# Group 0's keys as two transfers by slot, its first slot prepared and scored by itself, and keys ahead of queries in groups 1 and 2

## The chip, the cores and the metric

The kernel runs on one core of one Trainium2 chip. The metric is the device time of one execution in microseconds (us), the median of several runs. A time in the text without another name is a point on the clock of the profiled execution, counted from the start of its span.

## The reference, cut to what matters

Eight batches of twelve heads with 448 positions of 64 numbers go through a sigmoid attention. The result, seen as 3584 rows of 768, goes through two dense layers with a gated sigmoid between them. Inputs and output are fp32 in HBM.

```python
# q, k, v: (8, 12, 448, 64); w_in: (768, 2048); w_out: (2048, 768); beta: (2048,)
scores = q @ k.transpose(0, 1, 3, 2) / sqrt(64) - log(448)
attn   = sigmoid(scores) @ v                         # (8, 12, 448, 64)
x      = attn.transpose(0, 2, 1, 3).reshape(3584, 768)
h      = x @ w_in
g      = h * sigmoid(beta * h)
out    = g @ w_out                                   # (3584, 768)
```

## The kernel before, in words

**Groups, slots and tiles.** The twelve heads of a batch are worked in three groups of four heads (a "quad" in the code; groups 0, 1 and 2 are batch 0). The 128 partitions of a group's tile hold its four heads, 32 partitions each. A slot is a pair of heads, 64 partitions, so slot 0 of group 0 is the upper half of the tile and slot 1 the lower half. The 448 keys of a head are three key tiles of 128 (`jt` 0 to 2) and a last one of 64 (`jt` = `JF` = 3). In code, `NB` = 14 is the number of 32-position columns, `NH` = 7 is half of them, and `NF` = 12 is the columns of the three full tiles.

**Way of the data.** `load_one` (L106, its DMA at L110) brings a group's queries (`r` = 0) or keys (`r` = 1) by a DMA that GpSimd (POOL) issues and that casts to fp16 on the way. `transpose` (L186) has VectorE (DVE) transpose them in 32x32 blocks: queries at L191, the three full key tiles at L199, the last key tile at L203. `score` (L210, L213) multiplies them on TensorE (PE), `weigh` (L222, L224) applies the sigmoid on ScalarE (ACT), and `attend` (L270) multiplies with the values, which DVE casts out of PSUM at L290. `dense1` (L295) is the first dense layer: matmuls at L166 (the line of a helper for all dense matmuls), sigmoid at L307, product at L310. `dense2` (L321) is the second. The values come by `load_v` (L131 and L138), w_in in eight chunks by `load_w_in` (L148), w_out in four by `load_w_out` (L156). Chunk c of w_in holds what `dense1` needs for `dc` = 2c and 2c + 1. The first transfer of w_out serves parts 0 to 3 of the first `dense2`, that is its first eight matmuls, and the second transfer the next eight.

**The start, which the change touches.** Everything up to the first dense layer is in an order written out by hand (L509 on); each engine runs its instructions in that order. Group 0 is not cast by a DMA. SyncE (SP) issues two plain fp32 transfers at L519, the first half of the queries and then all keys, into a piece of the tile `gt` that is not yet in use. DVE casts the queries (L539) and transposes them; ACT casts the second half of the keys (L541) and DVE the first half (L542); DVE transposes all keys (L199, L203). Meanwhile PE multiplies zeros: `idle_units` (L533) issues matmuls of 512 columns whose result nobody reads, nine of them ahead of the first scores (L537), and four (two in the last group) between one half visit and the next (L563). A half visit (L252) is the scores of half of the queries of a group, for two slots: the first one of a group does key tiles 0 and 1 (16 matmuls, two sigmoids), the second one tile 2 and the last tile (16 matmuls, two sigmoids). Within a half visit the matmuls of the two slots alternate. There are three PSUM tiles for scores.

**POOL's order of transfers.** After a memset of `dummy` (L525): group 1's first query half, group 1's keys, the same two of group 2, four transfers of values (L131), two of values (L138), the second query half of group 0, that of group 1, chunks 0 to 3 of w_in, the second query half of group 2, chunks 4 to 7 of w_in. Later come group 3's queries and keys, two transfers of w_out and the values of batch 1. From the ninth transfer on, each one is issued only when the eighth one before it has landed, because eight semaphores take turns.

**After the start.** `attend`, `half_visit` and `fill_units` alternate (L564 on); `fill_units` takes the next units of the dense layers from a list. The transpose of group 2's second query half stands ahead of `attend(0, QH, QH)` in the code (L592), and the half visit that needs it, `half_visit(2, QH, 0)`, stands behind one dense unit (L594, L595).

Of the kernel before, what the change touches and what calls it, by code (L numbers as in the profile page):

```python
# [8 lines left out]
FP32 = mybir.dt.float32  # L9
FP16 = mybir.dt.float16  # L10
# [3 lines left out]
def kernel(  # L14
# [10 lines left out]
    nc = tc.nc  # L25
# [3 lines left out]
    B, H, S, D = q.shape  # L29
    NTOK, DM = out.shape  # L30
    DFF = moe_w_in.shape[1]
    P = 128
    BLK = 32
    HQ = P // BLK
    NB = S // BLK
    PAIR = D // BLK
    JF = S // P
    KL = S - JF * P
    NF = JF * P // BLK
    NPAIR = H // 2  # L40
    QPB = H // HQ
# [15 lines left out]
    kTp = ctx.enter_context(tc.tile_pool(name="kTp", bufs=4))  # L57
# [34 lines left out]
    dummy = const.tile([P, 1], FP32, name="dummy")  # L92
# [10 lines left out]
    raws = {}  # L103
    vs = {}

    def load_one(g: int, r: int, c0: int = 0, c1: int = NB):  # L106
        b, t = divmod(g, QPB)
        if g not in raws:
            raws[g] = rawp.tile([P, 2, NB, D], FP16, tag="raw", name="raw")
        nc.gpsimd.dma_start(  # L110
            out=raws[g][:, r, c0:c1].rearrange("p c d -> p (c d)"),
            in_=(q, k)[r][b, HQ * t : HQ * (t + 1)].rearrange("h (p c) d -> (h p) (c d)", c=NB)[
                :, c0 * D : c1 * D
            ],
        )
# [11 lines left out]
    def load_v(b: int):  # L127
        vs[b] = vp.tile([P, H, JF + 1, D], FP16, tag="v16", name="v16")
        rows = v[b].rearrange("h (p c) d -> p h (c d)", c=NB)
        for i in range(HQ):  # L130
            nc.gpsimd.dma_start(  # L131
                out=vs[b][i * BLK : (i + 1) * BLK, :, 0:JF].rearrange("p h j d -> p h (j d)"),
                in_=rows[:, :, JF * i * D : JF * (i + 1) * D],
            )
        rows = v[b].rearrange("h (p c) d -> p h c d", c=NB)
        for c in range(NF, NB):
            lo = (c - NF) * BLK
            nc.gpsimd.dma_start(out=vs[b][lo : lo + BLK, :, JF], in_=rows[:, :, c])  # L138

    def double_v_last(b: int):  # L140
        nc.vector.tensor_copy(out=vs[b][KL:P, :, JF], in_=vs[b][0:KL, :, JF])

    WCH = 8
    WOUT = 2

    def load_w_in(c: int):
        n = DFF // WCH
        nc.gpsimd.dma_start(  # L148
            out=w_in16[:, :, c * n : (c + 1) * n],
            in_=moe_w_in[:, c * n : (c + 1) * n].rearrange("(c p) f -> p c f", p=P),  # L150
        )
# [23 lines left out]
    kT = {}  # L175
# [6 lines left out]
    def in_order(b: int, t):  # L182
        t = t.rearrange("p c e -> p (c e)").bitcast(FP32)
        return t.rearrange("p (q c) -> p c q", c=NB) if b == B - 1 else t

    def transpose(g: int, r: int, c0: int = 0, c1: int = NB):  # L186
        raw = raws[g][:, r]
        if r == 0:
            if g not in qT:
                qT[g] = qTp.tile([P, NB * BLK, PAIR], FP16, tag="qT", name="qT")  # L190
            nc.vector.transpose(  # L191
                out=in_order(g // QPB, qT[g][:, c0 * BLK : c1 * BLK]),
                in_=raw[:, c0:c1].rearrange("p c d -> p (c d)").bitcast(FP32),
            )
            return
        kT[g] = kTp.tile([P, S, PAIR], FP16, tag="kT", name="kT")
        to = kT[g].rearrange("p k e -> p (k e)").bitcast(FP32)
        frm = raw.rearrange("p c d -> p (c d)").bitcast(FP32).rearrange("p (c f) -> p c f", c=NB)
        nc.vector.transpose(  # L199
            out=to[:, 0 : JF * P].rearrange("p (j i q) -> p i j q", j=JF, i=HQ),  # L200
            in_=frm[:, 0:NF].rearrange("p (i j) f -> p i j f", j=JF),
        )
        nc.vector.transpose(  # L203
            out=to[:, JF * P :], in_=frm[:, NF:].rearrange("p c f -> p (c f)")
        )

    def score_tile():
        return psum["sc"].tile([P, 2, 512], FP32, tag="sco", name="sco")

    def score(sco, u0: int, s: int, jt: int, hh: int, e: int, c0: int, n: int):  # L210
        g, lo = s // 2, (s % 2 * 2 + hh) * BLK
        base, nk = (last_base(s), KL) if jt == JF else (0, P)
        nc.tensor.matmul(  # L213
            sco[base : base + nk, hh, u0 : u0 + n],
            kT[g][lo : lo + BLK, jt * P : jt * P + nk, e],
            qT[g][lo : lo + BLK, c0 : c0 + n, e],
            start=(e == 0),
            stop=(e == PAIR - 1),
            tile_position=(lo, base),
        )  # L220

    def weigh(sco, n: int):  # L222
        at = attnp.tile([P, 2, S], FP16, tag="attnT", name="attnT")
        nc.scalar.activation(  # L224
            out=at[:, :, 0:n],
            in_=sco[:, :, 0:n],
            func=AF.Sigmoid,
            bias=NEG_LOG_S,
            scale=MSCALE,
        )  # L230
        return at
# [17 lines left out]
                at_tiles[s, jt, 0] = at  # L249


    def half_visit(g: int, c0: int, second: int):  # L252
        slots = (2 * g, 2 * g + 1)
        scos = [score_tile() for _ in slots]
        plan = [(s, jt, sco, jt * QH) for jt in (0, 1) for s, sco in zip(slots, scos)]
        widths = [S, S]
        if second:
            plan = [(s, 2, sco, 0) for s, sco in zip(slots, scos)]
            plan += [(s, JF, scos[0], QH) for s in slots]
            widths = [S, QH]  # L260
        for i in range(0, len(plan), 2):
            for e in range(PAIR):
                for s, jt, sco, u0 in plan[i : i + 2]:
                    for hh in range(2):
                        score(sco, u0, s, jt, hh, e, c0, QH)
        ats = {id(sco): weigh(sco, n) for sco, n in zip(scos, widths)}
        for s, jt, sco, u0 in plan:
            at_tiles[s, jt, c0] = ats[id(sco)][:, :, u0 : u0 + QH]
# [237 lines left out]
    NH = NB // 2  # L506
    firsts = ctx.enter_context(ExitStack())
    share_psum(firsts, 3, 2)
    with tc.manual_schedule():  # L509
        raws[0] = rawp.tile([P, 2, NB, D], FP16, tag="raw", name="raw")  # L510
        wide = gt.rearrange("p a b -> p (a b)").bitcast(FP32)
        cut = NH * D
        early = [(0, 0, NH), (1, 0, NB)]
        staged = {}
        at = 0
        for r, c0, c1 in early:
            staged[r] = wide[:, at : at + (c1 - c0) * D]
            at += (c1 - c0) * D
            nc.sync.dma_start(  # L519
                out=staged[r],  # L520
                in_=(q, k)[r][0, 0:HQ].rearrange("h (p c) d -> (h p) (c d)", c=NB)[
                    :, c0 * D : c1 * D
                ],
            )
        nc.gpsimd.memset(dummy, 0.0)  # L525
        nc.scalar.activation(out=dummy, in_=dummy, func=AF.Sigmoid, bias=0.0, scale=1.0)

        still = const.tile([P, 512], FP16, name="still")
# [4 lines left out]
        def idle_units(n: int):  # L533
            for _ in range(n):
                nc.tensor.matmul(idle, still[:, 0:P], still, start=True, stop=True)

        idle_units(9)  # L537
        raw = raws[0].rearrange("p r c d -> p r (c d)")
        nc.vector.tensor_copy(out=raw[:, 0, 0:cut], in_=staged[0])  # L539
        transpose(0, 0, 0, NH)  # L540
        nc.scalar.copy(out=raw[:, 1, cut:], in_=staged[1][:, cut:])  # L541
        nc.vector.tensor_copy(out=raw[:, 1, 0:cut], in_=staged[1][:, 0:cut])  # L542
        transpose(0, 1)
        for g in range(1, QPB):
            load_one(g, 0, 0, NH)
            load_one(g, 1)
        load_v(0)
        nc.sync.dma_start(out=beta_in[0:NDC], in_=moe_beta.rearrange("(c p) -> c p", p=P))
        for g in range(QPB - 1):
            load_one(g, 0, NH, NB)  # L550
        for c in range(WCH):
            if c == WCH // 2:
                load_one(QPB - 1, 0, NH, NB)
            load_w_in(c)
        for g in range(1, QPB):
            transpose(g, 0, 0, NH)
            transpose(g, 1)

        for g in range(QPB):
            for second in range(2):  # L560
                half_visit(g, 0, second)
                if 2 * g + second < 2 * QPB - 1:
                    idle_units(4 if g < QPB - 1 else 2)  # L563
        double_v_last(0)  # L564
        transpose(0, 0, NH, NB)
        attend(0, 0, QH)
        half_visit(0, QH, 0)
        attend(1, 0, QH)
        half_visit(0, QH, 1)
        for g in range(1, QPB - 1):  # L570
            transpose(g, 0, NH, NB)
# [128 lines left out]
```

## Time and profile before

| what | us |
|---|---|
| median of three runs | 383.44 |
| the three runs | 382.74 to 384.87 |
| the profiled execution | 383.27 |
| its span in the profile | 381.5 |
| PE busy | 375.9 (99% of the span) |
| DVE busy | 231.9 (61%) |
| ACT busy | 229.2 (60%) |
| POOL busy | 66.4 (17%) |

The span runs from the first instruction to the last; 1.77 us of the profiled execution lie around it. PE's busy time counts the matmuls on zeros as well. In a timeline row the first number is the start, the second the length, then engine, source line, operation, output and input tiles, shapes and how often; in brackets stands how long the engine had been idle and what ended that. A row that ends in x8 merges eight instructions of one kind, with the small gaps between them. PEld is TensorE's weight load, which runs beside its matmuls. SPq and POOLq are the queues that issue transfers.

### The profile page before, as it was taken

The page shows a single profiled execution, that of the slowest core. Times are in us where ns is not written, and L with a number is a line of the kernel's source. Part 1 is how long each engine was busy: PE and PEld are TensorE (multiplying, and loading weights), DVE is VectorE, ACT ScalarE, POOL GpSimd, SP SyncE. Part 2 cuts the span into 40 slices and gives each one's busy share as a digit, 9 for nine tenths or more (in the row PEclk, how much of TensorE's full clock was granted, in tenths as well). Part 3 has the DMA queues.
Part 4 walks back from the last instruction along what each step waited for, and adds up shares of the span by engine and source line. Part 5 has one row for each costly group of instructions (what it writes and reads, how often), then busy time and mean ns, then how long its engine had stood idle before and what let it go on. Part 6 is the DMA issues. An engine that isn't in the chain of part 4 may idle for free.

```text
span 381.5 us, 8227 instructions
## 1 busy us (share of the span) xinstructions
PE 375.9 (99%) x3415; PEld 199.0 (52%) x3415; DVE 231.9 (61%) x439; ACT 229.2 (60%) x330; POOL 66.4 (17%) x114
## 2 busy tenths in 40 slices
PE   8999999999999999999999999999999999999996
PEld 3477744444654445444554445544455444555563
DVE  4357366775765557465775657665676665755761
ACT  5987756687356776577355792477752787435100
POOL 7842433140110410040110410112100000000000
PEclk9999999999999999999999999999999999999999
DMA  9999999755363930672363850649203300030033
GB/s 169 187 197 205 192 204 210 164 71 54 50 132 84 121 51 2 131 98 24 50 132 72 115 69 2 133 87 117 50 0 84 85 1 2 2 83 0 2 83 125
DMA packets 42405, 34.71 MB, mean 91 GB/s; under 512 B 21872, under 2 KB 38656, under 8 KB 42368
## 3 DMA queue, kind: packets, MB, share of 16 engines
q0 software_dynamic: 36688, 22.47, 43.5%
q1 hardware_dynamic: 5680, 11.71, 11.6%
q8 instruction: 27, 0.44, 0.5%
q14 instruction: 10, 0.08, 0.1%
HBM read 45.62 MB, written 11.01 MB: 148 GB/s over the span
## 4 chain that ended last, share of the span: by engine, by line
PE 88%; DMA 9%; POOL 1%; issue 0%; DVE 0%; POOLq 0%
PE m_ps L166 70%; PE sco L213 10%; PE av_ps L281 8%; DMA w_out<-in_moe_w_out_dram 5%; DMA w_in<-in_moe_w_in_dram 3%; DMA raw<-in_k_dram 2%; POOL w_in L148 1%; POOL raw L110 1%; POOL w_out L156 0%; DVE osb L342 0%; POOL dummy L525 0%; POOLq L684 0%
## 5 line engine op out<-in xcount | busy, mean ns | idle before, releaser
L224 ACT ACTIVATE attnT<-sco 128x896 f16<-128x896 f32 (+1 forms) x171 | 145.3, 902 | 81.2 <-PE sco L213 80.6
L166 PE MATMUL m_ps<-xT,w_in 128*128 128x448 f16 (+2 forms) x1014 | 154.7, 336 | 0.1
L310 DVE TENSOR_TENSOR gt<-m_ps,sg 128x448 f16<-128x448 f32 (+1 forms) x144 | 81.4, 572 | 81.1 <-ACT sg L307 77.6
L166 PEld LDWEIGHTS <-w_in 128*128 128x128 f16 (+1 forms) x1014 | 82.6, 101 | 68.8 <-issue 15.0
L307 ACT ACTIVATE sg<-m_ps,beta_sb 128x448 f32<-128x448 f32 (+1 forms) x144 | 84.2, 597 | 36.5 <-PE m_ps L166 29.5
L166 PEld LDWEIGHTS <-sum 128*64 128x64 f16 (+1 forms) x664 | 48.0, 104 | 33.6 <-issue 7.9
L213 PE MATMUL sco<-qT,kT 32*128 32x448 f16 (+3 forms) x864 | 51.9, 340 | 0.7 <-DVE kT L199 0.6
L166 PE MATMUL m_ps<-w_T,sum 128*128 128x384 f16 (+1 forms) x360 | 51.6, 327 | 0.0
L110 POOL DMA_DIRECT2D raw<-in_q_dram x26 | 14.3, 552 | 184.1 <-DVE kT L203 176.9
L430 DVE TENSOR_TENSOR osb<-m_ps,osb 128x384 f32<-128x384 f32 x60 | 33.3, 555 | 18.7 <-PE m_ps L166 16.9
L166 PEld LDWEIGHTS <-gt 128*128 128x128 f16 (+1 forms) x414 | 31.4, 103 | 24.0 <-issue 6.5
L281 PE MATMUL av_ps<-attnT,v 128*64 128x448 f16 (+3 forms) x432 | 40.2, 338 | 0.0
L400 DVE TENSOR_TENSOR sum<-gt 128x1024 f16<-128x1024 f16 x60 | 39.2, 678 | 0.1
L290 DVE CAST xT<-av_ps 128x448 f16<-128x448 f32 (+1 forms) x54 | 28.5, 568 | 15.2 <-PE av_ps L281 14.1
L166 PE MATMUL m_ps<-w_T,gt 128*64 128x384 f16 (+1 forms) x268 | 34.3, 327 | 0.0
L166 PE MATMUL m_ps<-w_out,sum 128*64 128x384 f16 (+1 forms) x304 | 33.8, 327 | 0.0
L281 PEld LDWEIGHTS <-v 128*64 128x64 f16 (+1 forms) x432 | 20.6, 108 | 18.8 <-issue 9.4
L213 PEld LDWEIGHTS <-kT 32*128 32x128 f16 (+1 forms) x864 | 13.7, 96 | 28.6 <-issue 26.0
L166 PE MATMUL m_ps<-w_out,gt 128*128 128x384 f16 (+3 forms) x146 | 22.7, 327 | 0.1
L131 POOL DMA_DIRECT2D v<-in_v_dram x32 | 19.8, 631 | 9.6 <-DMA w_in<-in_moe_w_in_dram 5.2
L191 DVE STREAM_TRANSPOSE qT<-raw 128x448 f32<-128x448 f32 (+1 forms) x27 | 16.7, 617 | 0.1
L433 ACT COPY osb<-m_ps 128x384 f32<-128x384 f32 x12 | 5.8, 481 | 16.8 <-DMA out_dram<-osb 8.6
(25 smaller groups left out, 90.0 us busy)
## 6 DMA issues: line engine op xcount, KB each, us to landing
out_dram<-osb SPq DMA_DIRECT2D x98, 96.0 KB, 1.9
raw<-in_k_dram POOLq DMA_DIRECT2D x23, 224.0 KB, 4.9
raw<-in_q_dram POOLq DMA_DIRECT2D x21, 224.0 KB, 3.8
v<-in_v_dram POOLq DMA_DIRECT2D x32, 144.0 KB, 6.7
w_in<-in_moe_w_in_dram POOLq DMA_DIRECT2D x8, 384.0 KB, 11.2
w_out<-in_moe_w_out_dram POOLq DMA_DIRECT2D x4, 768.0 KB, 13.0
v<-in_v_dram POOLq DMA_DIRECT2D x16, 48.0 KB, 6.4
out_dram<-osb SPq DMA_DIRECT2D x2, 384.0 KB, 3.0
```

What stands on the lines that cost most here:

```text
L110: nc.gpsimd.dma_start(out=raws[g][:, r, c0:c1].rearrange("p c d -> p (c d)"), in_=(q, k)[r][b, HQ * t : HQ * (t + 1)].rearrange("h (p c) d ...
L131: nc.gpsimd.dma_start(out=vs[b][i * BLK : (i + 1) * BLK, :, 0:JF].rearrange("p h j d -> p h (j d)"), in_=rows[:, :, JF * i * D : JF * (i + ...
L166: nc.tensor.matmul(to[c : c + step], hidden[:, c : c + step], weights, **({} if step == P else {"tile_position": (0, c)}), **flags,)
L191: nc.vector.transpose(out=in_order(g // QPB, qT[g][:, c0 * BLK : c1 * BLK]), in_=raw[:, c0:c1].rearrange("p c d -> p (c d)").bitcast(FP32),)
L213: nc.tensor.matmul(sco[base : base + nk, hh, u0 : u0 + n], kT[g][lo : lo + BLK, jt * P : jt * P + nk, e], qT[g][lo : lo + BLK, c0 : c0 + n ...
L224: nc.scalar.activation(out=at[:, :, 0:n], in_=sco[:, :, 0:n], func=AF.Sigmoid, bias=NEG_LOG_S, scale=MSCALE,)
L281: nc.tensor.matmul(av[hh * D : (hh + 1) * D, 0:n], vs[b][base : base + nk, 2 * (s % NPAIR) + hh, jt], at[base : base + nk, hh, 0:n], start ...
L290: nc.vector.tensor_copy(out=xTs[b][:, s % NPAIR, c0 : c0 + n], in_=av[:, 0:n])
L307: nc.scalar.activation(out=sg[:, 0:n], in_=m1[:, 0:n], func=AF.Sigmoid, bias=0.0, scale=beta_sb[:, dc : dc + 1])
L310: nc.vector.tensor_tensor(out=gt[:, dc, off : off + n], in0=m1[:, 0:n], in1=sg[:, 0:n], op=ALU.mult)
L400: nc.vector.tensor_tensor(out=sums[t, i], in0=x, in1=y, op=op)
L430: nc.vector.tensor_tensor(out=out, in0=in0, in1=in1, op=op)
```

## The change

The first part concerns group 0. SP now issues three transfers, the queries' first half, the keys of slot 0 (64 partitions) and the keys of slot 1. The casts and transposes of the keys are cut into pieces: ACT casts key tiles 0 and 1 of slot 0 and tile 0 of slot 1, DVE casts tile 1 of slot 1, then tile 2 and the last tile of both slots, with the transposes between. In the first half visit of group 0 all scores of slot 0 come ahead of those of slot 1, and one idle unit stands between them. The idle units at the start become eight, and the four behind the first half visit become two. The memset of `dummy` moves from POOL to DVE.

The second part is the order of POOL's transfers: keys ahead of the queries in groups 1 and 2, and the second query half of group 2 behind chunk 4 of w_in instead of ahead of it. DVE's transposes of groups 1 and 2 follow: full key tiles, queries, last key tile. The instructions behind these places keep their order on every engine.

```diff
+    def transpose_keys(g: int, j0: int, j1: int, rows):
+        if g not in kT:
+            kT[g] = kTp.tile([P, S, PAIR], FP16, tag="kT", name="kT")
+        to = kT[g][rows].rearrange("p k e -> p (k e)").bitcast(FP32)
+        frm = raws[g][rows, 1].rearrange("p c d -> p (c d)").bitcast(FP32)
+        frm = frm.rearrange("p (c f) -> p c f", c=NB)
+        if j0 == JF:
+            nc.vector.transpose(
+                out=to[:, JF * P :], in_=frm[:, NF:].rearrange("p c f -> p (c f)")
+            )
+            return
         nc.vector.transpose(
+            out=to[:, j0 * P : j1 * P].rearrange("p (j i q) -> p i j q", i=HQ, q=BLK),
+            in_=frm[:, 0:NF].rearrange("p (i j) f -> p i j f", j=JF)[:, :, j0:j1],
         )
...
-    def half_visit(g: int, c0: int, second: int):
+    def half_visit(g: int, c0: int, second: int, between=None):
...
-        for i in range(0, len(plan), 2):
+        if between:
+            plan = [x for sco in scos for x in plan if x[2] is sco]
+        step = 1 if between else 2
+        for i in range(0, len(plan), step):
+            if i == 2 and between:
+                between()
             for e in range(PAIR):
-                for s, jt, sco, u0 in plan[i : i + 2]:
+                for s, jt, sco, u0 in plan[i : i + step]:
...
+        by_slot = [slice(x * P // 2, (x + 1) * P // 2) for x in range(2)]
+        nc.sync.dma_start(
+            out=flat(q0),
+            in_=q[0, 0:HQ].rearrange("h (p c) d -> (h p) (c d)", c=NB)[:, 0 : NH * D],
+        )
+        for x, rows in enumerate(by_slot):
             nc.sync.dma_start(
+                out=flat(k0[rows]),
+                in_=k[0, 2 * x : 2 * x + 2].rearrange("h (p c) d -> (h p) (c d)", c=NB),
+            )
-        nc.gpsimd.memset(dummy, 0.0)
+        nc.vector.memset(dummy, 0.0)
...
-        idle_units(9)
+        idle_units(8)
...
-        nc.scalar.copy(out=raw[:, 1, cut:], in_=staged[1][:, cut:])
-        nc.vector.tensor_copy(out=raw[:, 1, 0:cut], in_=staged[1][:, 0:cut])
-        transpose(0, 1)
+        cast_keys(nc.scalar.copy, by_slot[0], 0, 2)
+        transpose_keys(0, 0, 2, by_slot[0])
+        cast_keys(nc.scalar.copy, by_slot[1], 0, 1)
+        cast_keys(nc.vector.tensor_copy, by_slot[1], 1, 2)
+        transpose_keys(0, 0, 2, by_slot[1])
+        every = slice(0, P)
+        cast_keys(nc.vector.tensor_copy, every, 2, JF)
+        nc.vector.tensor_copy(out=raw_k[:, NF:], in_=k0[:, NF:])
+        transpose_keys(0, 2, JF, every)
+        transpose_keys(0, JF, JF + 1, every)
         for g in range(1, QPB):
+            load_one(g, 1)
             load_one(g, 0, 0, NH)
-            load_one(g, 1)
...
         for c in range(WCH):
-            if c == WCH // 2:
+            if c == WCH // 2 + 1:
                 load_one(QPB - 1, 0, NH, NB)
             load_w_in(c)
         for g in range(1, QPB):
+            transpose_keys(g, 0, JF, every)
             transpose(g, 0, 0, NH)
-            transpose(g, 1)
+            transpose_keys(g, JF, JF + 1, every)
...
-                half_visit(g, 0, second)
+                first = 2 * g + second == 0
+                half_visit(g, 0, second, (lambda: idle_units(1)) if first else None)
                 if 2 * g + second < 2 * QPB - 1:
-                    idle_units(4 if g < QPB - 1 else 2)
+                    idle_units(2 if first else 4 if g < QPB - 1 else 2)
```

More of the change, by code (lines that the diff above doesn't have):

```diff
@@ L195, in transpose @@
             return
[L196 to L204, printed above, removed]
+        transpose_keys(g, 0, JF, slice(0, P))
+        transpose_keys(g, JF, JF + 1, slice(0, P))
+    def transpose_keys(g: int, j0: int, j1: int, rows):
[9 more added lines that the diff above has]
+            return
+        nc.vector.transpose(
+            out=to[:, j0 * P : j1 * P].rearrange("p (j i q) -> p i j q", i=HQ, q=BLK),
+            in_=frm[:, 0:NF].rearrange("p (i j) f -> p i j f", j=JF)[:, :, j0:j1],
         )
@@ L511, with flat @@
         wide = gt.rearrange("p a b -> p (a b)").bitcast(FP32)
[L512 to L518, printed above, removed]
+        k0 = wide[:, 0 : NB * D].rearrange("p (c d) -> p c d", c=NB)
+        q0 = wide[:, NB * D : (NB + NH) * D].rearrange("p (c d) -> p c d", c=NH)
+        def flat(t):
+            return t.rearrange("p c d -> p (c d)")
+        by_slot = [slice(x * P // 2, (x + 1) * P // 2) for x in range(2)]
[4 more added lines that the diff above has]
+        for x, rows in enumerate(by_slot):
             nc.sync.dma_start(
[L520 to L523, printed above, removed]
+                out=flat(k0[rows]),
+                in_=k[0, 2 * x : 2 * x + 2].rearrange("h (p c) d -> (h p) (c d)", c=NB),
             )
-        nc.gpsimd.memset(dummy, 0.0)
+        nc.vector.memset(dummy, 0.0)
         nc.scalar.activation(out=dummy, in_=dummy, func=AF.Sigmoid, bias=0.0, scale=1.0)
@@ L535, in idle_units, with by_tile, cast_keys @@
                 nc.tensor.matmul(idle, still[:, 0:P], still, start=True, stop=True)
-        idle_units(9)
-        raw = raws[0].rearrange("p r c d -> p r (c d)")
-        nc.vector.tensor_copy(out=raw[:, 0, 0:cut], in_=staged[0])
-        transpose(0, 0, 0, NH)
-        nc.scalar.copy(out=raw[:, 1, cut:], in_=staged[1][:, cut:])
-        nc.vector.tensor_copy(out=raw[:, 1, 0:cut], in_=staged[1][:, 0:cut])
-        transpose(0, 1)
+        idle_units(8)
+        raw_q, raw_k = raws[0][:, 0], raws[0][:, 1]
+        def by_tile(t, rows, j0: int, j1: int):
+            return t[rows, 0:NF].rearrange("p (i j) d -> p i (j d)", j=JF)[:, :, j0 * D : j1 * D]
+        def cast_keys(copy, rows, j0: int, j1: int):
+            copy(out=by_tile(raw_k, rows, j0, j1), in_=by_tile(k0, rows, j0, j1))
+        nc.vector.tensor_copy(out=raw_q[:, 0:NH], in_=q0)
+        transpose(0, 0, 0, NH)
+        cast_keys(nc.scalar.copy, by_slot[0], 0, 2)
[8 more added lines that the diff above has]
+        transpose_keys(0, JF, JF + 1, every)
         for g in range(1, QPB):
+            load_one(g, 1)
             load_one(g, 0, 0, NH)
-            load_one(g, 1)
         load_v(0)
```

## Prediction

> **What bounds the kernel now.** I read the page's chain of work first. It ends in PE almost everywhere, but a tenth of it is transfers:
>
> ```profile
> PE 88%; DMA 9%; POOL 1%; issue 0%; DVE 0%; POOLq 0%
> ```
>
> The chain cut to the first 60 us tells where these transfers stand (start, length, what):
>
> ```profile
> 2.96 6.43 DMA raw<-in_k_dram
> ...
> 12.70 10.47 DMA w_in<-in_moe_w_in_dram
> 23.18 0.28 issue
> 23.46 0.88 POOL w_out L156
> 24.34 18.36 DMA w_out<-in_moe_w_out_dram
> 42.71 0.04 issue
> 42.75 1.46 PE m_ps L166 x8
> ```
>
> The second transfer of w_out lands at 42.71, and PE goes on at 42.75. From there to the end the chain is PE without a gap, so a shift of the matmuls at 42.75 is the shift of the end. Ahead of 42.7 transfers set the pace. The DMA share by stretches is 0.93 or more in every microsecond from 2 to 5, and at 18.36 us from issue to landing this transfer waited in a long queue. The timelines of POOL, PEld and DVE from 24 to 30 us show a gate on the way:
>
> ```profile
> 25.20 0.40 DVE L191 STREAM_TRANSPOSE qT<-raw 128x224 f32<-128x224 f32 x1
> 26.13 0.59 PE L213 MATMUL sco<-qT,kT 32*128 32x224 f16 x16
> 26.33 0.62 POOL L131 DMA_DIRECT2D v<-in_v_dram  x1 [1.10 <-DMA w_in<-in_moe_w_in_dram]
> 28.03 0.50 PEld L166 LDWEIGHTS <-w_in 128*128 128x128 f16 x6 [0.30 <-DMA w_in<-in_moe_w_in_dram]
> 28.27 0.62 POOL L131 DMA_DIRECT2D v<-in_v_dram  x1 [1.32 <-DMA w_in<-in_moe_w_in_dram]
> ```
>
> POOL's rows are clocks for landings, since each waits for the transfer eight before it and resumes 0.28 later (the issue piece at 23.18). So w_in's chunk 3 landed at 23.17, chunk 4 at 26.33 - 0.28 = 26.05, chunk 5 at 27.99, and PE waited for chunk 5 (28.03).
>
> **How much PE is early at the gates.** Thirty dense matmuls from 33.61 to 36.59 give 0.0993 each. Chunk 3 is needed 12 matmuls after 22.02, at 23.21: 0.04 after landing. Chunk 5 is needed 12 matmuls after 26.66, at 27.85: PE stood 0.18. At 42.75 eight w_out matmuls had begun at 41.17 and take 1.46 as in the chain's last row, so PE stood 42.75 - 42.63 = 0.12. A start that gets faster runs into chunk 3's landing and keeps 0.04; one that gets slower is forgiven 0.18 and 0.12.
>
> **Part one: group 0 by slots.** The start of before, on PE, DVE and ACT:
>
> ```profile
> 1.19 4.02 PE L535 MATMUL idle_ps<-still 128*128 128x512 f16 x9 [1.19 <-DVE still L529]
> ...
> 4.54 0.56 ACT L541 CAST raw<-gt 128x448 f16<-128x448 f32 x1 [2.31 <-DMA gt<-in_k_dram]
> 4.54 0.45 DVE L542 CAST raw<-gt 128x448 f16<-128x448 f32 x1 [0.29 <-DMA gt<-in_k_dram]
> 5.13 0.58 DVE L199 STREAM_TRANSPOSE kT<-raw 128x384 f32<-128x384 f32 x1
> 5.64 0.20 DVE L203 STREAM_TRANSPOSE kT<-raw 128x64 f32<-128x64 f32 x1
> 5.76 0.44 PEld L213 LDWEIGHTS <-kT 32*128 32x128 f16 x16 [1.46 <-DVE kT L199]
> 5.77 0.69 PE L213 MATMUL sco<-qT,kT 32*128 32x224 f16 x16 [0.56 <-DVE kT L199]
> 6.40 1.04 PE L535 MATMUL idle_ps<-still 128*128 128x512 f16 x4
> 7.37 0.80 PE L213 MATMUL sco<-qT,kT 32*128 32x224 f16 x16
> ```
>
> The keys are 448 KB at 4.54. Slot 0 is half of it; at the 361 GB/s of the stretch 3 to 4 us that half is 0.64 us, so it lands at 3.90 if the halves move one after the other, and at 4.54 at the latest if they move together. Slot 1 lands between 4.54 and 4.98, later by up to one issue of SP (0.44, two SP rows apart); I take 4.65. No row has the new shapes, so I scale with elements, and the bounds are the rows' own values. ACT's cast of 512 columns, 0.62 (0.56 for 448): to 4.52. DVE's transpose of 256, 0.45 (between 0.41 for 224, L191, and 0.58 for 384): to 5.0. Slot 0's eight matmuls, 0.55 (0.35 is half the row of 16; 0.8 if two instead of four run side by side): to 5.6. For slot 1 DVE casts 256 (0.26; at most 0.45) to 5.3, ACT's cast is over by 5.05, DVE transposes to 5.75, and PE scores to 6.35, the idle unit being over by then. Tile 2 and the last tile cost DVE two casts (0.26, 0.20) and two transposes (0.28, 0.20): ready at 6.75, while PE does its two idle units (0.52) to 6.9. The second half visit begins at 6.95 instead of 7.37: **0.4 gained**, bounds -0.3 (both halves together, DVE's pieces at their upper ends) and +0.6. What follows there is the same sequence of scores and idle matmuls. Groups 1 and 2 hide their reordered transposes: group 1's keys now come first of the pair, whose second landed at 7.45 (DVE's wait at L199); full tiles 0.58 before it, then queries 0.41 and last tile 0.20, ready at 8.1 against scores at 8.65. Values (13.61) and group 0's second query half (14.00) are used by PE from 15.2 on and cover 0.4 too. ACT moves along: its sigmoids wait for these scores. Chunk 3's gate then takes the gain, all but 0.04.
>
> **Part two: POOL's stream.** The memset (0.10) and the pause behind it (0.42) stand ahead of POOL's first transfer at 1.26. Without them it starts between 0.73 and 1.26, so the stream shifts by at most 0.53. But at 2 to 4 us the transfers already move 299 and 361 GB/s, above all later stretches; only the stretch 1 to 2 us (38 GB/s) has room. On the other side SP's third transfer may hold the stream up by 0.44. I take 0.1 earlier, being nearest to the full stretches. The bytes ahead of chunk 5 and of w_out are unchanged, so these gates move by 0.1 only.
>
> Group 2's second query half now lands behind chunk 4. Chunk 3 to 4 is 2.88, chunk 4 to 5 is 1.94, so that transfer is 0.94 long and landed at 24.1 or so; it will land where chunk 4 did, 26.05, and chunk 4 at 25.1. Its transpose ran at 25.20, in the shade of other work. It can't begin before 26.05: end 26.45, scores at 26.55 instead of 26.13. **PE loses 0.42**. Behind it on DVE wait two casts of L290 and a product of L310 (0.69 and 0.39), which free PSUM banks; PE waits at the scores anyway. Chunk 5's gate gives 0.18 back, w_out's 0.12.
>
> **The sum.** 0.42 - 0.18 - 0.12 - 0.1 = +0.02 at 42.75, with the start's gain spent at chunk 3. On the profiled execution's 383.27 (span 381.5 and 1.77 around it; 0.17 under the median, inside the runs' 382.74 to 384.87) that is **383.3**.
>
> **What pages say against it.** The Trainium skill (DMA: Bandwidth & Descriptors, Rules for kernel authors) advises one transfer of 128 partitions instead of two to disjoint halves, since both halves use the same engines. The rows can't show it, as no transfer here is split so; by it there is no gain in the last landing, and at worst the rival "together" below. The Trainium skill (TensorE: Matmul & The Clock Gate, Part 1) has TensorE at half rate until some 3.4 us of sustained work are over, in a window that runs freely; the rows agree that it begins slow: nine idle matmuls in 4.02 us, later four in 1.04.
>
> **Rivals.**
> (a) The stream really starts 0.53 earlier. For: POOL's pause of 0.42. Against: the full stretches. The gates move by 0.53, the late query half too: 0.42 - 0.18 - 0.12 - 0.53, or 382.9. If the query half comes out earlier than I infer, PE's early arrival binds: 382.8.
> (b) The halves land together, or slot 1 late. The start loses up to 0.3; PE reaches 26.13 late, by less than the 0.42 that it waits there anyway: 383.3 to 383.5. The change then doesn't do what it says.
> (c) Slower: PE's clock rises late. An idle matmul takes 0.45 (4.02/9) early and 0.26 (1.04/4) later; in before the rise came during the scores that began at 5.77, after a pause of 0.56. With eight units work ends at 1.3 + 3.6 = 4.9; if the scores start after about 5.5, or slot 1's later than 6.3, the pauses are longer than that. The decision is whether idle matmuls behind the first scores take 0.26 or 0.45. A second slow stretch like the first (4.02) does half its work, 2.0; less 0.4, 0.18, 0.12 and 0.1: 384.5. Against: the pauses I work out are shorter than 0.56. Two such stretches would be 386.5.
> (d) The gates aren't gates, and the start's 0.4 comes through: with the stream, 382.8. Against: 28.03.
>
> **How the numbers follow.** Forecast 0.55, (a) 0.16, (b) 0.10, (c) 0.11, (d) 0.08. The range takes in the stream's bounds (383.3 - 0.43 to 383.3 + 0.54), (a), (d) and (c)'s first stretch, and below the lowest run of before (0.53 under the profiled one): 382.3 to 384.5; left out are two slow stretches and what I haven't seen. 0.5% is 1.9 us, about what a measurement of this kernel can tell from no change. Only (c) with a second stretch, 0.05, is slower by that; faster by that needs a stream 1.9 us earlier, which nothing here gives, 0.04; 0.91 stays within.
>
> **What would show it.** Right: first scores near 5.05, second half visit near 6.95, PE waiting at chunk 3 (about 23.1), the transpose of group 2's second half near 26.0 with PE waiting behind it, w_out near 42.6. Wrong: w_out's landing moved by more than 0.5 either way, PE no longer standing at any transfer, or idle matmuls of 0.45 behind the first scores.

## The result, and the profile after

| | before | after |
|---|---|---|
| median of the runs of one session, us | 383.96 (6 runs) | 386.95 (6 runs) |
| profiled execution, us | 383.27 | 386.92 |
| its span, us | 381.5 | 385.1 |

The changed kernel is slower: ratio 1.0091, 95% interval 1.0069 to 1.0113, that is 2.6 to 4.3 us. (The medians of the table differ by 3.0: three of the six runs of before lie above 384.) The forecast was no change, 383.3, with 384.5 as the upper end.

The page's chain of work, in the line that answers to the first one shown of before, no longer holds transfers of w_in and w_out:

```profile
PE 97%; DMA 1%; ACT 0%; DVE 0%; SPq 0%; issue 0%
```

The chain of the changed kernel cut to the first 60 us (start, length, what) says what took their place:

```profile
1.18 5.23 DMA gt<-in_k_dram
6.41 0.02 issue
6.43 0.63 ACT raw L560
7.06 0.02 issue
7.08 0.45 DVE kT L210
7.53 0.05 issue
7.57 0.93 PE sco L221 x8
...
11.88 1.47 PE idle_ps L551 x4
...
44.01 3.86 PE m_ps L166 x28
47.87 0.51 PE sco L221 x8
```

Slot 0's keys, half the bytes of before, land at 6.41 instead of 4.54 for all keys. From the first scores at 7.57 the chain is PE up to the last copy of a result, but for one sigmoid at 17.10: no transfer holds PE up any more, because PE is late for all of them. ACT's row for slot 1 shows the second landing, 7.86:

```profile
7.88 0.40 ACT L560 CAST raw<-gt 64x256 f16<-64x256 f32 x1 [0.84 <-DMA gt<-in_k_dram]
```

The scores behind the first `dense2` begin at 47.87; in before's chain they are the piece at 44.21. That is 3.66 later, and the span is 3.6 longer, so the whole loss stands already there.

The timeline of PE in the start shows a second thing:

```profile
1.22 3.60 PE L551 MATMUL idle_ps<-still 128*128 128x512 f16 x8 [1.22 <-DVE still L545]
7.57 0.93 PE L221 MATMUL sco<-qT,kT 32*128 32x224 f16 x8 [2.75 <-DVE kT L210]
8.44 0.61 PE L551 MATMUL idle_ps<-still 128*128 128x512 f16 x1
8.97 0.93 PE L221 MATMUL sco<-qT,kT 32*128 32x224 f16 x8
9.83 1.03 PE L551 MATMUL idle_ps<-still 128*128 128x512 f16 x2
10.80 1.07 PE L221 MATMUL sco<-qT,kT 32*128 32x224 f16 x16
11.81 1.54 PE L551 MATMUL idle_ps<-still 128*128 128x512 f16 x4
13.28 0.58 PE L221 MATMUL sco<-qT,kT 32*128 32x224 f16 x16
13.79 1.04 PE L551 MATMUL idle_ps<-still 128*128 128x512 f16 x4
```

After a pause of 2.75 PE runs slowly: two idle matmuls take 1.03, as long as four take from 13.79 on. The second half visit begins at 10.80 instead of 7.37 (3.43 late); the scores that wait for a sigmoid begin at 18.07 instead of 13.89 (4.18 late), although two idle matmuls were taken out. First before, then after:

```profile
13.89 0.69 PE L213 MATMUL sco<-qT,kT 32*128 32x224 f16 x14 [0.18 <-ACT attnT L224]
```

```profile
18.07 0.69 PE L221 MATMUL sco<-qT,kT 32*128 32x224 f16 x14 [0.18 <-ACT attnT L232]
```

### The profile page after: what moved, and what is told of

The parts are those of the page before. It is cut to its first block, busy times and chain, and to the rows that moved or that the text cites. A ratio compares the mean times of both kernels' runs of the same rounds, so it can differ in the third digit from the quotient of the medians.

```text
span 385.1 us, 8231 instructions
## 1 busy us (share of the span) xinstructions
PE 377.6 (98%) x3413; PEld 199.6 (52%) x3413; DVE 232.7 (60%) x444; ACT 229.8 (60%) x331; POOL 66.3 (17%) x113
## 4 chain that ended last, share of the span: by engine, by line
PE 97%; DMA 1%; ACT 0%; DVE 0%; SPq 0%; issue 0%
PE m_ps L166 74%; PE sco L221 12%; PE av_ps L294 9%; DMA gt<-in_k_dram 1%; PE idle_ps L551 1%; ACT attnT L232 0%; ACT raw L560 0%; DVE kT L210 0%; DVE osb L355 0%; SPq L532 0%
## 5 line engine op out<-in xcount | busy, mean ns | idle before, releaser
L221 PE MATMUL sco<-qT,kT 32*128 32x448 f16 (+3 forms) x864 | 53.4, 344 | 2.9 <-DVE kT L210 2.8
L210 DVE STREAM_TRANSPOSE kT<-raw 128x384 f32<-128x384 f32 (+2 forms) x26 | 14.1, 543 | 3.0 <-ACT raw L560 2.8
```

The lines of the kernel that those rows point to most:

```text
L221: nc.tensor.matmul(sco[base : base + nk, hh, u0 : u0 + n], kT[g][lo : lo + BLK, jt * P : jt * P + nk, e], qT[g][lo : lo + BLK, c0 : c0 + n ...
```

## The experiments

Theories after the result: **S**, the split itself makes group 0's keys late; **O**, POOL's new order does; and part of the loss is PE's slow **clock** (matmuls at half their later rate). Times are medians; "ref" is the kernel before, run on the same chip beside them.

### The split alone, the order alone, and each taken out of the change

Split alone, on the kernel before:

```diff
-            nc.sync.dma_start(out=staged[r], in_=...)
+            for lo, hi in ((0, P),) if r == 0 else ((0, P // 2), (P // 2, P)):
+                nc.sync.dma_start(out=staged[r][lo:hi], in_=...)
```

> The kernel before with one edit: group 0's keys come in two transfers of 64 partitions, everything else (casts, transposes, scores, POOL's order) as before. Theory S (the split itself makes group 0's keys land late): the casts of the keys at L541/L542 begin at 7 to 8 us instead of 4.54, PE's clock rises late, and the time is 2.5 to 4 us above the kernel before. Theory O (POOL's keys-first order makes them late, by its larger packets beside group 0's): the casts begin at 4.5 to 5.0 and the time is within 0.6 us of the kernel before.

Measured: 386.99 against 383.19, ratio 1.0097 (1.0072 to 1.0123). Its ACT timeline:

```profile
7.42 0.57 ACT L542 CAST raw<-gt 128x448 f16<-128x448 f32 x1 [5.19 <-DMA gt<-in_k_dram]
```

Casts at 7.42 instead of 4.54, and the whole loss of the change: S holds.

Order alone, on the kernel before (DVE's transposes of groups 1 and 2 follow that order):

```diff
-            load_one(g, 0, 0, NH)
             load_one(g, 1)
+            load_one(g, 0, 0, NH)
```

> The kernel before with one edit: in groups 1 and 2 POOL loads keys ahead of queries, and DVE transposes them in that order. Theory S: group 0's keys land at 4.5 to 4.7 as before, time within 0.6 us of the kernel before. Theory O: the casts of group 0's keys begin after 6 us and the time is 2 us or more above the kernel before.

Measured: 384.39 against 383.19, ratio 1.0019 (0.9997 to 1.004). The casts begin at 4.79, 0.25 later than before. O falls as the main cause. The time is not within the 0.6 that S asked for, by medians: seven of twelve runs lie above 384, against seven of 23 of ref. The profiled run is one of the lower ones, so it doesn't show why.

The change with the old order (the same lines turned back):

> The changed kernel with POOL's old order for groups 1 and 2 (queries ahead of keys), the split and all else kept. Theory S: slot 0's cast still begins at 6 us or later and the time stays 2.5 to 4 us above the kernel before. Theory O: slot 0's cast begins near 4 us, the second half visit near 7, and the time is within 0.8 us of the kernel before. Both at work: in between, slot 0 near 5.

Measured: 386.62, ratio 1.0081 (1.0059 to 1.0102). Slot 0's cast begins at 5.32 (6.43 in the change), slot 1's at 7.30 (7.88). The order moves slot 0 by about 1 us, between the two expectations, but PE needs slot 1 as well, and the time is that of the change.

The change with one transfer:

```diff
-        for x, rows in enumerate(by_slot):
-            nc.sync.dma_start(out=flat(k0[rows]), in_=...)
+        nc.sync.dma_start(out=flat(k0), in_=...)
```

> The changed kernel with group 0's keys in one transfer of 128 partitions; the casts, transposes and scores by slot and POOL's new order are kept. Theory S: ACT's first cast begins near 4.55, the second half visit near 7.4 to 7.8, and the time is within 0.8 us of the kernel before. Theory O: the cast begins after 6 us and the time is 2 us or more above the kernel before.

Measured: 385.9, ratio 1.0043 (1.0021 to 1.0065), single runs from 383.12 to 386.57. The cast begins at 4.78 as S says, yet the second half visit begins at 9.15 and the time misses the expectation. PE's timeline shows why:

```profile
5.93 0.93 PE L221 MATMUL sco<-qT,kT 32*128 32x224 f16 x8 [1.11 <-DVE kT L210]
...
10.16 1.89 PE L550 MATMUL idle_ps<-still 128*128 128x512 f16 x4
```

A pause of 1.11, and after it four idle matmuls in 1.89: the clock is late with keys that come only 0.24 later than before.

### The clock by itself

The change with more idle matmuls at the start:

```diff
-        idle_units(8)
+        idle_units(14)
```

> The changed kernel with 14 instead of 8 idle matmuls ahead of the first scores; they end near 7 us and fill PE's pause of 2.75 us. Theory of the clock (part of the loss is that PE runs slowly until 12.9 us, because the keys come late and PE pauses): idle matmuls behind the first scores take 0.26 instead of 0.45, the 0.75 us by which PE falls further behind between the second half visit (3.43 late) and the matmuls at 18.07 (4.18 late) goes, and the time falls by 0.5 to 1.0 us. Rival (PE waits for DVE's pieces and the sigmoids, its rate matters little): less than 0.3 us.

Measured: 384.77, ratio to ref 1.0045 (1.0024 to 1.0066), about 2.2 under the change. PE's timeline:

```profile
1.22 5.66 PE L551 MATMUL idle_ps<-still 128*128 128x512 f16 x14 [1.22 <-DVE still L545]
7.48 0.57 PE L221 MATMUL sco<-qT,kT 32*128 32x224 f16 x8 [0.60 <-DVE kT L210]
...
9.48 0.70 PE L221 MATMUL sco<-qT,kT 32*128 32x224 f16 x16
10.11 1.04 PE L551 MATMUL idle_ps<-still 128*128 128x512 f16 x4
```

Slot 0's keys come as late as in the change (first scores at 7.48 against 7.57), but every row behind them is at the full rate, and the second half visit begins at 9.48 instead of 10.80. The clock is worth about 2 us, twice what I expected at most; slot 1's cast begins at 7.50 instead of 7.88 in this run, so up to 0.4 of it may be the landing's. The rest, 1.6 over ref, holds the late keys: this run's chain begins with their second transfer, landing at 7.48.

The granted clock of the profile (PEclk, the third figure from the right) shows the slow stretch in some traces. The microsecond 9 to 10 of the split alone, where four idle matmuls take 1.89, and of the change, where two take 1.03:

```profile
9.00:10.00 1.00, 1.00 (x18) 0.36 (x7) 1.00 (x5) 0.37 (x1) 0.48 (x2) 0.50 1.57 186
```

```profile
9.00:10.00 1.00, 1.00 (x10) 0.52 (x10) 1.00 (x5) 0.52 (x2) 0.44 (x2) 1.00 1.59 189
```

With the split alone, and with POOL held back below, it falls to 0.50; there some of the nine idle matmuls ahead of the pause had been fast already (nine in 3.96, 3.60 and 3.81 instead of before's 4.02). In the change all eight were slow (3.60), so the rate had not risen before the pause, and the column reads 1.00, as it does over the slow start of before. For the change, then, the slow clock is read from the length of the matmuls.

The kernel before with eight and with ten instead of nine:

> The kernel before with eight instead of nine idle matmuls ahead of the first scores, which makes PE's pause before them about 1.0 instead of 0.56 us; the keys land as before. Theory of the clock: a longer pause lets PE's rate come late more often, so that the time is 0.5 to 2 us above the kernel before, and idle matmuls behind the first scores take 0.45 in the profile. Rival (the rate was lost only because the keys came 2 to 3 us late): within 0.4 us of the kernel before, idle matmuls of 0.26.

Measured: 384.06, ratio 1.001 (0.9996 to 1.0024), which is no clear difference of the whole. But six of twelve runs lie above 384 (six of 29 of ref beside them), and the profiled one, with a pause of 1.27, has four idle matmuls in 1.89.

> The kernel before with ten instead of nine idle matmuls ahead of the first scores, so that PE goes on nearly without a pause. Theory of the clock: the runs of the kernel before near 384.6 are those in which PE's rate came late; with ten they go, and the median falls by up to 0.5 us, to 382.9, with no run above 384. Rival: the two clusters of the kernel before have another cause and stay.

Measured: 383.02 against 383.10, ratio 0.9992 (0.998 to 1.0004); none of twelve runs is above 384. With ten idle matmuls the pause is 0.38, and no run near 384.6 is seen, as the clock theory says. None of twelve against six of 29 could be chance; over all sessions 23 of 94 runs of ref lie above 384. That a run of that cluster of nine idle matmuls has a slow clock is inferred, since the profiled run of before is of the lower cluster.

### Why the split keys land late

Theories: **C**, the keys' packets now leave when POOL's stream begins, and the two share the engines; **G**, a transfer of 64 partitions is slow in itself. The split with POOL held back by a memset, once for 2.02 and once for 3.94 us:

```diff
         nc.gpsimd.memset(dummy, 0.0)
+        nc.gpsimd.memset(w_out16[:, 0:3], 0.0)    # 0:6 in the longer one
```

> The kernel before with group 0's keys in two transfers of 64 partitions (as in the run with the split alone), and a memset on POOL (of a part of w_out's tile, overwritten later) ahead of its first transfer, so that POOL's stream begins about 2 to 3 us later. Theory C: with nothing else moving, the casts of the keys begin at 4.9 or sooner. Theory G: they begin after 6 us as with the split alone. The whole time is no measure here: every transfer of POOL comes later, so it may be 2 to 3 us above the kernel before under both.

> As the run with the two transfers of 64 partitions and POOL held back, but held about twice as long (4 us), so that group 0's keys move alone. Theory C (POOL's stream beside them is the whole delay): the casts begin at 5.0 or sooner. Theory G (a part of the delay is the second transfer's own): 5.3 or later. The whole time is no measure, since all of POOL's transfers come late.

Measured: casts at 5.64 and at 5.76 (385.11 and, in a single run, 386.25; POOL's late stream may be part of both). ACT's row in the longer one, where POOL's first transfer is issued at 4.65:

```profile
5.76 0.56 ACT L543 CAST raw<-gt 128x448 f16<-128x448 f32 x1 [3.52 <-DMA gt<-in_k_dram]
```

Neither theory alone: of the 2.9 us by which the split is late (7.42 against 4.54), 1.7 go when POOL's stream is away, and 1.2 stay. The Trainium skill (DMA: Bandwidth & Descriptors, Queues, rings and completion order) says that each engine takes turns, packet by packet, between the queues that have work; the 1.7 agree, and in the change both queues move packets in each microsecond from 3 to 8. The timelines of SP's queue, before and after, give part of the 1.2:

```profile
1.18 0.42 SPq L519 DMA_DIRECT2D gt<-in_k_dram  x1
```

```profile
1.18 1.19 SPq L537 DMA_DIRECT2D gt<-in_k_dram  x2
```

All keys are issued by 2.37 instead of 1.60, 0.77 later. The other 0.4 stays open. It is not a lack of transfer rate: in the longer hold, the DMA engines are busy for 0.01 of the microsecond from 5 to 6, at 4 GB/s (the last two figures), and the cast begins only at 5.76:

```profile
5.00:6.00 1.00, 0.00 (x1) 0.00 (x0) 0.62 (x2) 0.24 (x1) 1.00 (x3) 1.00 0.01 4
```

Two transfers by columns, each of all 128 partitions:

```diff
+            for lo in range(c0, c1, NH):
+                nc.sync.dma_start(out=staged[r][:, (lo - c0) * D : (lo - c0 + NH) * D], in_=...)
```

> The kernel before with group 0's keys in two transfers by columns: each has all 128 partitions and half of the row, 1792 bytes, as the queries' transfer has. Theory of the shape (64 partitions are what makes it slow): casts begin at 4.5 to 5.0, time within 0.6 us of the kernel before. Theory of the count (a second transfer on SP's queue is what makes it late, whatever its shape): the casts of the second half begin after 6 us and the time is 2 us or more above the kernel before.

Measured: 387.22, ratio 1.0106 (1.009 to 1.0121). The first half is there by 4.12, where DVE casts it without a wait; ACT's cast of the second half begins at 7.66 after a wait for its transfer. The shape is not it: a second transfer is late in either shape.

Slot 1 issued by ScalarE:

```diff
-            nc.sync.dma_start(
+            (nc.sync, nc.scalar)[x].dma_start(
                 out=flat(k0[rows]),
```

> The changed kernel with slot 1's keys issued by ScalarE instead of by SyncE behind slot 0's. Theory C (the second issue behind the first goes out late, 1.19 us for both rows, and the keys' packets then meet POOL's stream): slot 1 lands at 5.0 to 6.0 instead of 7.86 and slot 0 below 5, time 1 to 2.5 us below the changed kernel. Theory G (a transfer of 64 partitions is slow in itself): landings at 6.4 and 7.9 within 0.5, time within 0.5 us of the changed kernel.

Measured: 388.63, ratio 1.0139 (1.0124 to 1.0155). Both theories missed the time. The queries' cast begins at 4.18 (3.41), slot 0's at 7.06 (6.43): with a third queue beside theirs both landed later, which neither theory had. ACT casts slot 1 behind slot 0 without a wait, so that cast doesn't show slot 1's landing; its 0.23 MB, on a queue of their own, moved from 2 to 5 us (0.09, 0.13 and 0.01 in the three), which fits C. So slot 1 was early and slot 0 late, and the kernel needs slot 0 first.

### The second query half of group 2

Only that transfer moved behind chunk 4, on the kernel before (`c == WCH // 2 + 1`):

> The kernel before with one edit: group 2's second query half is loaded behind chunk 4 of w_in. The prediction's step: the transpose of that half begins near 26.0 instead of 25.20, the scores behind it begin near 26.55 instead of 26.13, and what is left after the later gates is 0.1 us. Rival (the half lands before PE gets there, or the transposes wait without PE waiting): scores at 26.1 or earlier. In both cases the time is within 0.6 us of the kernel before.

Measured: 383.12 against 383.10, ratio 1.0004 (0.9988 to 1.002). DVE's and PE's timeline:

```profile
25.56 0.75 PE L166 MATMUL m_ps<-xT,w_in 128*128 128x224 f16 x6
25.84 0.41 DVE L191 STREAM_TRANSPOSE qT<-raw 128x224 f32<-128x224 f32 x1 [0.49 <-DMA raw<-in_q_dram]
...
26.30 0.57 PE L213 MATMUL sco<-qT,kT 32*128 32x224 f16 x16
```

DVE's wait is there, and the scores begin 0.17 late (26.30 against 26.13), between the two expectations. But 0.11 of that stands already in the row ahead (25.56 against 25.45 in before), which this transfer doesn't touch, so the half itself costs PE some 0.06. Behind the next gate nothing is left: the scores at 29.29 in before begin at 29.22.

### What is left without the two causes

The change with one transfer and `idle_units(10)`, and the same with POOL's old order:

> The changed kernel with group 0's keys in one transfer and ten idle matmuls ahead of the first scores: neither of the two causes found so far is left, only the preparation and scoring by slot. Theory of the two causes: idle matmuls behind the first scores take 0.26, time within 0.5 us of the kernel before (383.1). Rival (the pieces by slot cost time themselves, DVE having more and shorter instructions on the way): the second half visit still begins after 8.5, and the time is 0.7 to 1.5 us above the kernel before.

> The same with POOL's old order (queries ahead of keys in groups 1 and 2). Theory: the order of POOL's transfers matters only beside a split transfer of group 0's keys, so the time is within 0.4 us of the run with the new order. Rival: 0.5 us or more apart.

Measured: 383.75, ratio 1.0016 (0.9999 to 1.0033), and 383.26, ratio 0.9994 (0.998 to 1.0007), both against 383.10. They are 0.49 apart, between the two expectations for the order, and the first is 0.65 over ref where 0.5 was expected at most. PE's timeline of the first:

```profile
5.98 0.57 PE L221 MATMUL sco<-qT,kT 32*128 32x224 f16 x8 [0.68 <-DVE kT L210]
...
7.90 0.70 PE L221 MATMUL sco<-qT,kT 32*128 32x224 f16 x16
8.53 1.04 PE L550 MATMUL idle_ps<-still 128*128 128x512 f16 x4
```

The second half visit at 7.90 is 0.5 behind before's 7.37, so the pieces by slot don't make the start faster, but the time is that of the kernel before. What is left over doesn't stem from the start, as this run's chain shows:

```profile
26.17 16.79 DMA w_out<-in_moe_w_out_dram
```

It holds PE up again, landing at 42.96 instead of before's 42.71. With POOL's old order no transfer of w_in or w_out is in the chain, and the second half visit, at 7.72, is still 0.35 behind before's. No version that ran beats it by a clear margin.

## Why the prediction was wrong, point by point

- **The failed step: "lands at 3.90 if the halves move one after the other, and at 4.54 at the latest if they move together. Slot 1 lands between 4.54 and 4.98".** Measured 6.41 and 7.86. I bounded the landings by the keys' own bytes and by SP's issue, and asked for POOL's stream only whether it would come earlier. The keys of before were through just as that stream began: SP's queue had moved 0.69 of its 0.70 MB by 4.0 us, in the change 0.37. I took 0.44 for an issue of SP where the keys' two took 1.19, and what else is in the 1.2 that stay with POOL away had no term in my sum. The windows of the two kernels, 3 to 4 us (last column GB/s), first before, then after:

```profile
3.00:4.00 1.00, 1.00 (x4) 0.32 (x3) 0.56 (x2) 0.00 (x0) 1.00 (x2) 1.00 1.01 361
```

```profile
3.00:4.00 1.00, 1.00 (x4) 0.36 (x3) 0.55 (x2) 0.00 (x0) 1.00 (x2) 1.00 0.73 124
```

  The 361 GB/s with which I priced the half were the rate of a transfer that had the engines nearly to itself (POOL's packets took 10% of the engines' time); in the change the same microsecond has 124, with the engines busy for only 0.73 of it, so sharing is a part of the loss and not all.
- **The rival "together" took breaking the rule of one 128-partition transfer as nearly harmless** (383.3 to 383.5). The rule was right, and breaking it cost 2.9 us of landing with the split alone, 1.2 with POOL away.
- **Rival (c), the late clock, had the right mechanism and price and too small a chance.** Its deciding point was first scores after about 5.5; they came at 7.57. It priced one slow stretch at 2.0; taking the slow clock away gave about 2 back. Its 386.5 for two such stretches is near the measured time by luck: the trace has one further stretch, from 7.57 to about 13, and the rest is late keys, which that sum doesn't have. I gave it 0.11 because I held the pause to be shorter than 0.56, which hung on the landing above. It also needed no late keys: one transfer with eight idle matmuls had it too. The Trainium skill (TensorE: Matmul & The Clock Gate, Part 1) has the rate fall back after an idle window of some 3.4 us and ties the windows to no event of the kernel; no run here shows an idle window of that length being needed: in the profiles idle matmuls were slow after every pause of 1.11 or more, and after none of 0.38 to 0.92, and with POOL held back the granted clock fell to 0.50 after pauses of 1.99 and 2.09. What the runs can't tell is where a window began.
- **The gates.** PE was so late that none held: 4.18 late at the wait for a sigmoid, 3.95 behind chunk 5's gate (33.24 against 29.29), 3.66 at 47.87, behind w_out's. So the start's lateness came through but for 0.23 and 0.28, against my 0.18 and 0.12: the gates were there, w_out's more than twice as wide as I had it.
- **Late query half: 0.42 forecast, some 0.06 measured alone** (0.17 at the scores, 0.11 of it from ahead), since the half landed at about 25.8 and not 26.05. In the change itself it never showed: PE was later than the transfer, and the transpose ran at 29.38 without a wait.
- **POOL's stream: 0.1 earlier forecast, 0.02 measured** at the first issue (1.24 against 1.26). The pause of 0.42 was not the memset's. Further on the stream fell back: w_out's first transfer was issued at 24.78 instead of 23.46, which cost nothing because PE was later still.
- **The slot-wise start: 0.4 gain forecast.** With one transfer and a full clock the second half visit is 0.5 later than before. Slot 0's transpose waits for ACT's cast of 0.62, and behind it DVE's casts and transposes of slot 1, tile 2 and the last tile follow one after the other up to the second half visit.

Together: the ratio 1.0091 is 3.5 us. By medians of several sessions, 386.95 to 383.10 is 3.85: 2.2 went with PE kept busy (to 384.77), 1.0 with one transfer instead of two and ten idle matmuls (to 383.75), and the last 0.65 is a difference whose interval (0.9999 to 1.0033) doesn't exclude nothing. By the ratios, each to its own ref, the three are 1.8, 1.1 and 0.6. In the profiles the scores behind the first `dense2` begin at 47.87, 45.70, 44.46 and, in before, at 44.21: 2.2, 1.2 and 0.25.

## What to carry to other kernels

A landing is bounded not by the transfer's own bytes alone: ask which other queue starts in the same microsecond, and whether the transfer is through before. A piece that arrives earlier helps only if the last piece does not arrive later, and the last of two transfers was later in both shapes tried. Filler work that keeps PE warm must reach nearly up to the first real matmul (here a pause of 0.92 did no harm and one of 1.11 did), so when a wait ahead of it grows, the filler has to grow with it, not shrink.

## What the runs showed of the hardware

- SP's issue of a 64-partition transfer took 0.55 to 0.59 (two in 1.19; one in 0.56 where ScalarE issued the other, in 0.55), of a 128-partition one 0.38 to 0.43. It may not be the shape alone: the issue of beta behind them took 0.58 with the 64-partition transfers and 0.43 without, in the same shape.
- Runs about 1.5 us higher were six of twelve with eight idle matmuls ahead of the first scores, none of twelve with ten and six of 29 with nine. Eight against ten is hardly chance; nine against either could be.
- The granted clock fell to 0.50 behind pauses of 1.99 to 3.50, and read 1.00 in slow stretches in which the rate had not yet risen.
- While POOL's memset of 3.94 us ran, DVE's first cast took 1.55 instead of 0.39 (3.40 to 4.95); the shorter one was over at 2.8, and the cast behind it took 0.39.
